# An S4D convolution beside a 16-head attention on one core: weights loaded by kind, one set of seeds kept on chip, step sizes multiplied in by diagonals

## The chip, the cores and the metric

The kernel runs on one core of one Trainium2 chip, in one launch. The metric is the device time in microseconds (us); where a kernel was run several times it is the median. The core's engines have short names throughout: PE (TensorE, the matrix unit, whose weight loads are listed apart as PEld), DVE (VectorE), ACT (ScalarE), POOL (GpSimd) and SP (SyncE, which issues most DMAs). [...]

## What is computed

Two independent results for a sequence of L = 2048 positions and D = 448 channels are put side by side.

```python
def _A_ref(u, log_A_real, A_imag, C_real, C_imag, log_dt, D_skip):     # N = 256 states per channel
    dt = jnp.exp(log_dt)
    A = -jnp.exp(log_A_real) + 1j * A_imag
    C = (C_real + 1j * C_imag) * dt[:, None]
    P = jnp.exp((A * dt[:, None])[:, :, None] * pos[None, None, :])
    K = 2.0 * jnp.einsum("dn,dnl->dl", C, P).real
    # y = causal convolution of u with K along L, by FFTs of 2 L
    return y + u * D_skip
def _B_ref(x, wqkv, wo):                                               # H = 16 heads of 28
    q, k, v = split(x @ wqkv)
    p = softmax(q k^T * 28 ** -0.5)
    return (p v) @ wo
out = concatenate([_A_ref(...), _B_ref(...)], axis=-1)
```

## The kernel before

All matmuls of the projections and scores run in fp32r on pairs of numbers, a rounded part ("hi") and its remainder ("lo"), so that three products (hi hi, hi lo, lo hi) come close to fp32. Every engine call goes through one helper (line 75), so the profile shows the same line for all instructions and is read by tiles. Up to the main loop a scheduler decides the order of the instructions; in the main loop they keep the order in which the program issues them (`KEPT`, lines 87, 93 and 903).

**Projections and seeds** (lines 226 to 575). The 448 columns of x are cut into four slices of 112 (`CK`, `NCK`). For each of four chunks of 512 rows, `transposes` turns x on PE (tile `pt`), ACT writes the rounded part `xh`, DVE the remainder `xl`. `qk_proj` makes eight products per chunk (four head groups, K and Q) and `v_proj` four, each of 4 slices x 3 matmuls into one PSUM tile `pm`; ACT and DVE then write hi and lo (`hl`, for Q of the last chunk into `xn`), which go to DRAM. The weights come in four DMAs, one per slice, with Q, K and V side by side (`tri`, lines 305 to 311); ACT and DVE split them into hi and lo, in the space that K of group 0 takes later (`w_g` in `k0_t`, tile `khat`).

Between the projections run the seeds of the convolution, `seeds(o)`, for eight sets of 56 channels. A set's four parameter blocks land in `nat` (56 x 4 x 256); ACT takes the exponential of the first and multiplies all four with the step sizes (`times_dt`, one instruction each); `turn` transposes them in eight pieces into one PSUM tile `pn`; phases, sizes and sines follow (tile `tri`), then powers of the states in `se` (stored from a buffer of tile `qhat`, 896 KB a set) and `sg` (1456 KB a set). `factors` ends with negated copies, three ACT instructions per call, two calls a set. `put_e` and `put_g` store a set to DRAM (`sd`). The stores of set 6 (`kept_e`, `kept_g`) are issued after the last projection, around the loads of v and of q.

**First maxima** (lines 576 to 589). The softmax needs a row maximum for each query. For the first unit of queries (head group 0, chunk 0) 16 groups of four matmuls are made here, into five PSUM tiles; ACT takes a relu of one per group, DVE the maxima. `max_end` turns the result (tile `mh`) and `max_put` writes it with two DMAs into two spare rows of `q_u[0]`, so that the score matmul subtracts the maximum by itself. These two DMAs are on ACT's queue.

**Hand-over** (lines 903 to 910). Three loads of `sdb` (one channel block of 336 KB each) are issued, one on ACT's queue, then the maxima of the first three groups of the next unit (`LEAD` = 3, twelve matmuls through three PSUM tiles), called the lead here, then the first seeds are copied (`k_seeds`).

**Main loop** (lines 1045 to 1102). 256 steps: 16 units of 512 queries by one head group, 16 blocks of 128 keys. `ORDER` (line 34) writes out what a step issues: four score matmuls `s` (tile `pss`, exponentials on ACT into `p`), four maxima matmuls `m` for the step 19 ahead, the product with v of the step before (`pv`, tile `po`), slots `f` for the convolution, and `v` and `k`, which build the convolution's kernel from the seeds (`e_power` on POOL, `g_powers` on DVE, block b from step 3.5 b on). K of the next head group is loaded in four pieces at steps 1, 5, 9 and 13 of a group's second unit (line 1066), into `k0_p` and `kq_p` by turns.

Of the kernel before, what the change touches and what calls it, by code (L numbers as in the profile page):

```python
# [17 lines left out]
L = 2048  # L18
D = 448
# [8 lines left out]
CK = 112  # L28
NCK = D // CK
# [12 lines left out]
SGB, XB, XL = 2, 5, 4  # L42
# [10 lines left out]
NO = 8  # L53
BO = NB // NO
# [36 lines left out]
def body(ctx, tc, a, out):  # L91
# [50 lines left out]

    kt_g, kd_g, q_u, m_u, mh_u, o_u, rl_u = {}, {}, {}, {}, {}, {}, {}
# [82 lines left out]
    with ExitStack() as st:  # L226
        sst, xst, wst = ExitStack(), ExitStack(), ExitStack()
        t_p = pool(sst, "t_p")
# [19 lines left out]
        def load_nat(o, queue=nc.sync):  # L248
            nats[o] = s_p.tile([PO, 4, 256], F32, name="nat", bufs=2)
# [4 lines left out]
        dt_all = s_p.tile([PO, 5, NO], F32, name="dt_all")  # L254
        small = s_p.tile([128, BO, SDF - F_G], F32, name="sg", bufs=SGB)
# [6 lines left out]
        load_nat(0, nc.scalar)  # L262
# [27 lines left out]
        def turn_dt():  # L290
            dt_ps = ps_t.tile([128, CQ], F32, name="pt")[:PO, :NO]
            nc.tensor.transpose(dt_ps, dt_o, ident[:NO, :NO])
            for i, f in enumerate((1.0, 0.15915494309189535, 2.0, -2.0, -1.0)):
                nc.vector.tensor_scalar(dt_all[:, i, :], dt_ps, f, None, op0=ALU.mult)

        load_x(0)
        w_g = k0_t[:CK].rearrange("p g (i s k h e) -> p i s k g h e", i=2, s=2, k=NCK, h=HG)
        vh = y_p.tile([CK, NCK, D], F32R, name="vh")
        vl = y_p.tile([CK, NCK, D], F32R, name="vl")
        nc.gpsimd.memset(k0_t[:CK].rearrange("p g (n e) -> p (g n) e", e=32)[:, :, DH:].bitcast(F32), 0.0)  # L300
# [5 lines left out]
        for i in range(2):  # L306
            wn = t_p.tile([128, 3, LV, BO * 16], F32, name="tri", bufs=2).rearrange("p t k h -> p (t k h)")
            wn = wn[:CK, :2 * 3 * D].rearrange("p (k s d) -> p k s d", k=2, s=3)
            wns += [wn[:, 0], wn[:, 1]]
        for k in range(NCK):  # L310
            nc.sync.dma_start(wns[k], wqkv[k * CK:(k + 1) * CK, :].rearrange("p (s d) -> p s d", s=3))
# [5 lines left out]
        for k in range(NCK):  # L317
            for s in (1, 0):
                src = wns[k][:, s, :].rearrange("p (g h e) -> p g h e", g=G, e=DH)
                hi, lo = (w_g[:, i, s, k, :, :, :DH] for i in range(2))  # L320
                nc.scalar.activation(hi, src, AF.Copy)
                nc.vector.tensor_tensor(lo, src, hi.bitcast(F32), ALU.subtract)
            nc.scalar.activation(vh[:, k, :], wns[k][:, 2, :], AF.Copy)
            nc.gpsimd.tensor_tensor(vl[:, k, :], wns[k][:, 2, :], vh[:, k, :].bitcast(F32), ALU.subtract)
# [6 lines left out]
        def seeds(o):  # L331
# [53 lines left out]
            def places():  # L385
                se = q_p.tile([128, HG, CQ], F32R, name="qhat", bufs=3).bitcast(F32).rearrange("p h q -> p (h q)")
                q["se"] = se = se[:, :BO * F_G].rearrange("p (b f) -> p b f", f=F_G)
                q["sg"] = sg = s_p.tile([128, BO, SDF - F_G], F32, name="sg", bufs=SGB)
                q["e8"] = se.rearrange("p b (c h e) -> p b c h e", c=2, e=8)
# [779 lines left out]
```

## Time and profile before

| | us |
|---|---|
| median of 3 runs (1276.06 to 1277.42) | 1276.75 |
| the profiled execution | 1278.37 |
| its span, first to last instruction | 1276.6 |
| PE busy in the span | 1223.9 |
| DVE, ACT, POOL busy | 923.0, 967.5, 846.2 |

The profile is of one execution. A row of a group gives engine, operation, output and input tiles with their shapes and the count, then busy time and mean duration in ns, then the engine's idle time before these instructions and who ended it. A row of the timeline gives start, duration, engine, operation and tiles, with an idle time before it in brackets. The granted clock is the share of full speed that PE's clock had. Matmuls overlap in the array, so that their pace is read from their starts and not from their durations.

### The profile page before, as it was taken

The numbers are of one execution on the slowest core, as the hardware profiler recorded it, in microseconds if no ns is written. First come the engines' busy times: TensorE is split into PE (matmuls) and PEld (weight loads), VectorE is DVE, ScalarE is ACT, GpSimd is POOL, SyncE is SP. The second block draws the span as 40 slices with busy tenths as digits, with TensorE's granted clock in tenths as the row PEclk, the third lists the DMA queues.
The fourth block names the chain that finished last, engine by engine and source line by source line (L and its number), as shares of the span: only waits on it lengthen the run. The fifth ranks groups of instructions, "written<-read, shape, count | busy, mean of one in ns | idle before, by whom it ended". The sixth has DMA issues, their size and how long they took to land.

```text
span 1276.6 us, 33328 instructions
## 1 busy us (share of the span) xinstructions
PE 1223.9 (96%) x12641; PEld 699.3 (55%) x12641; DVE 923.0 (72%) x2106; ACT 967.5 (76%) x2162; POOL 846.2 (66%) x728
## 2 busy tenths in 40 slices
PE   7789887999999999999999999999999999999997
PEld 5667664555555555555555555555555545544433
DVE  6788866877777877877788888888897645645111
ACT  6878765788888888888878888888887666656452
POOL 2666750897788888878599999989995222324321
PEclk9889999899999999999999999999999999999999
DMA  7768699446564645375633133422324533657666
GB/s 216 244 223 288 233 304 346 113 93 186 160 149 113 168 119 168 113 235 167 176 94 104 49 88 97 154 81 71 88 54 156 179 131 135 204 170 228 198 170 167
DMA packets 200089, 205.36 MB, mean 161 GB/s; under 512 B 95992, under 2 KB 158520, under 8 KB 197880
## 3 DMA queue, kind: packets, MB, share of 16 engines
q1 hardware_dynamic: 199400, 202.63, 52.6%
q8 instruction: 100, 1.64, 0.5%
q10 hardware_dynamic: 528, 0.59, 0.2%
q14 instruction: 61, 0.50, 0.1%
HBM read 120.73 MB, written 82.18 MB: 159 GB/s over the span
## 4 chain that ended last, share of the span: by engine, by line
PE 75%; DVE 8%; POOL 6%; ACT 4%; issue 3%; DMA 3%; SPq 0%; ACTq 0%; POOLq 0%; DVEq 0%
PE pm L75 43%; PE pss L75 16%; PE po L75 16%; POOL e L75 2%; DVE tri L75 1%; ACT rl L75 1%; POOL qhat L75 1%; DVE mx L75 1%; DVE sg L75 1%; POOL eu L75 1%; ACT tri L75 1%; DVE px L75 1%; DVE qhat L75 1%; DVE hl L75 1%; DMA sd<-qhat 1%
## 5 line engine op out<-in xcount | busy, mean ns | idle before, releaser
L75 ACT ACTIVATE p<-pss 128x512 f32<-128x512 f32 x1024 | 561.0, 610 | 112.5 <-PE pss L75 107.2
L75 PE MATMUL pss<-qhat,khat 128*128 128x512 f32 x1024 | 403.2, 400 | 1.5 <-ACT p L75 1.4
L75 DVE TENSOR_REDUCE mx<-pm 128x1 f32<-128x512 f32 x480 | 308.6, 684 | 109.1 <-PE pm L75 107.2
L75 PE MATMUL pm<-khat,qhat 128*128 128x512 f32 x749 | 325.9, 438 | 6.4 <-ACT rl L75 4.2
L75 POOL TENSOR_TENSOR e<-e,sdb 128x256 f32<-128x256 f32 x168 | 201.8, 1201 | 110.6 <-ACT e L75 101.2
L75 PE MATMUL po<-p,v 128*32 128x512 f32 x2048 | 269.1, 594 | 0.0
L75 POOL TENSOR_TENSOR e<-e,eu 128x256 f32<-128x256 f32 x168 | 248.2, 1477 | 13.2
L75 PEld LDWEIGHTS pm<-khat,qhat 128*128 128x128 f32 x749 | 141.0, 189 | 201.9 <-ACT p L75 47.8
L75 DVE CUSTOM_DVE_ANT_0 rl<-pm,rl 128x512 f32<-128x512 f32 x259 | 178.3, 689 | 72.1 <-ACT rl L75 69.1
L75 PEld LDWEIGHTS pss<-qhat,khat 128*128 128x128 f32 x1024 | 190.6, 189 | 46.7 <-issue 10.8
L75 POOL TENSOR_TENSOR eu<-e,sdb 128x256 f32<-128x256 f32 x168 | 201.9, 1202 | 0.0
L75 POOL TENSOR_TENSOR p<-pr,pr 64x448 f32<-64x448 f32 x64 | 73.2, 1144 | 158.2 <-PE pm L75 132.8
L75 ACT ACTIVATE rl<-pm 128x512 f32<-128x512 f32 x259 | 156.6, 606 | 14.0 <-PE pm L75 8.4
L75 DVE TENSOR_TENSOR g<-g,zg 128x128 f32<-128x128 f32 x392 | 162.2, 414 | 3.4
L75 PE MATMUL pm<-kdif,qhat 128*128 128x512 f32 x249 | 100.5, 403 | 4.3 <-DVE xn L75 2.4
L75 PE MATMUL pm<-xh,khat 112*128 112x512 f32 x256 | 87.3, 425 | 4.9 <-DVE hl L75 1.8
L75 DVE TENSOR_TENSOR zg<-g,zg 128x128 f32<-128x128 f32 x224 | 88.0, 393 | 5.1
L75 PEld LDWEIGHTS pm<-e,g 128*32 128x32 f32 x3584 | 57.2, 109 | 43.4 <-issue 17.1
L75 DVE TENSOR_TENSOR pr<-pm,ub 128x448 f32<-128x448 f32 x64 | 37.0, 620 | 56.4 <-PE pm L75 42.0
L75 PE MATMUL pm<-e,g 128*32 128x64 f32 x3584 | 73.0, 222 | 1.8 <-POOL e L75 1.8
L75 ACT ACTIVATE y<-pm 128x448 f32<-128x448 f32 x48 | 26.5, 553 | 58.2 <-PE pm L75 36.2
L75 ACT ACTIVATE ub<-pm 128x224 f32<-128x224 f32 (+1 forms) x96 | 38.8, 449 | 39.7 <-PE pm L75 37.3
(134 smaller groups left out, 1461.8 us busy)
## 6 DMA issues: line engine op xcount, KB each, us to landing
sdb<-sd SPq DMA_DIRECT2D x55, 336.0 KB
qhat<-q SPq DMA_DIRECT2D x64, 256.0 KB
khat<-k SPq DMA_DIRECT2D x64, 256.0 KB
sd<-sg SPq DMA_DIRECT2D x8, 1456.0 KB
k<-hl SPq DMA_DIRECT2D x16, 512.0 KB
mw<-in_mw SPq DMA_DIRECT2D x16, 512.0 KB
sd<-qhat SPq DMA_DIRECT2D x8, 896.0 KB
yu_d<-ub SPq DMA_DIRECT2D x64, 112.0 KB
```

The costliest lines, as they stand in the source:

```text
L75: i = f(*args, **kw)
```

## The change

- The slices become three of 128 columns and one of 64 (`CK`, `TL`). In the last slice the 64 columns stand twice: x and its weights are loaded into both halves, DVE turns the lower half of `xh` into remainders, and so `w_hi` and `w_lo` times that tile are two matmuls and no third.
- The weights are loaded by kind, K first, then Q, then V, five DMAs each, and split in that order ahead of the jobs of the first chunk, whose four K projections stand first.
- The seeds' sets run in the order 1 to 7, 0. Set 0 stays in SBUF, in a tile `k1_p` of K's size that is allocated from the start (it replaces the odd groups' place in `kq_p` and holds `nat`, `sg` and the diagonals meanwhile); its seven blocks are read from there, and neither stored nor loaded. The stores of set 7 and three loads of v stand behind the row of maxima, which is now on SP's queue. Loads of the next K come 8 steps later (`KL`).
- The lead's matmuls stand behind the row too, in twelve allocations over `pm`, `pt`, `pn` and `px`, and step 0 has an order of its own.
- `times_dt` keeps one ACT multiplication (the phases); DVE makes four diagonals `dg` of step sizes, and `turn` multiplies three blocks by them while turning: fp32 products in the place of six transposes.
- The three negated copies of `factors` are one instruction.

```diff
-CK = 112
-NCK = D // CK
+CK = 128
+NCK = 4
+TL = D - 3 * CK
+ORDER_0 = ('s0', 's1', 's2', 'k', 's3', 'm0', 'm1', 'v', 'f', 'f', 'v', 'm2', 'm3', 'v')
+KL = 8
-SGB, XB, XL = 2, 5, 4
+XB, XL = 5, 3
+SETS = (1, 2, 3, 4, 5, 6, 7, 0)
+ORDER_QK = tuple((g, s) for g in range(4) for s in (1, 0))
...
+        k1_f = k1_p.tile([128, HG * L], F32, name="khat")
+        n_g, n_n = BO * (SDF - F_G), 4 * 256
+        sg_at = (0, HG * L - n_g)
...
-                xns[c, h] = y_p.tile([128, 2, CQ], F32, name="xn", bufs=3)[:, :, :D]
-                nc.sync.dma_start(xns[c, h], xs[:, 2 * h:2 * h + 2, :])
+                xns[c, h] = y_p.tile([128, 2, CQ], F32, name="xn", bufs=3)
+                for d, n, at in ((0, D, 0), (D - TL, TL, D)):
+                    nc.sync.dma_start(xns[c, h][:, :, at:at + n], xs[:, 2 * h:2 * h + 2, d:d + n])
...
-        for k in range(NCK):
-            nc.sync.dma_start(wns[k], wqkv[k * CK:(k + 1) * CK, :].rearrange("p (s d) -> p s d", s=3))
+        for s in (1, 0, 2):
+            for k in range(NCK):
+                for p in range(1 if k < NCK - 1 else 2):
+                    n = CK if k < NCK - 1 else TL
+                    nc.sync.dma_start(wns[s][p * TL:p * TL + n, k], wqkv[k * CK:k * CK + n, s * D:(s + 1) * D])
...
-            def times_dt(i):
-                n, d = q["nat"][:, i, :], dt_all[:, i or 4, o:o + 1]
-                act.activation(n, n, AF.Copy, scale=d)
+            def times_dt():
+                n = q["nat"][:, 1, :]
+                act.activation(n, n, AF.Copy, scale=dt_all[:, 1, o:o + 1])
+                vec.tensor_tensor(dg, ident[:PO, None, :PO].to_broadcast([PO, 4, PO]),
+                                  dt_all[:, :, o][:, :, None].to_broadcast([PO, 4, PO]), ALU.mult)
...
-                        nc.tensor.transpose(ps[:, i, :, h, :], q["nat"][:, i, h * 128:(h + 1) * 128], ident[:PO, :PO])
+                        n = q["nat"][:, i, h * 128:(h + 1) * 128]
+                        if i == 1:
+                            nc.tensor.transpose(ps[:, i, :, h, :], n, ident[:PO, :PO])
+                        else:
+                            nc.tensor.matmul(ps[:, i, :, h, :], n, dg[:, i].rearrange("p (b e) -> p b e", e=8), start=True, stop=True)
...
-                for k in range(i, i + 3):
-                    act.activation(zz[:, k, :, n_, :], zz[:, k, :, p_, :], AF.Copy, scale=-1.0)
+                act.activation(zz[:, i:i + 3, :, n_, :], zz[:, i:i + 3, :, p_, :], AF.Copy, scale=-1.0)
...
-                xl[k] = x_p.tile([CK, CQ], F32R, name="xl", bufs=XL)
-                nc.vector.tensor_tensor(xl[k], pt, xh[k].bitcast(F32), ALU.subtract)
+                if k < NCK - 1:
+                    xl[k] = x_p.tile([CK, CQ], F32R, name="xl", bufs=XL)
+                    nc.vector.tensor_tensor(xl[k], pt, xh[k].bitcast(F32), ALU.subtract)
+                else:
+                    nc.vector.tensor_tensor(xh[k][TL:], pt[TL:], xh[k][TL:].bitcast(F32), ALU.subtract)
...
-                for i, x_ in ((0, xh), (1, xh), (0, xl)):
+                for i, x_ in ((0, xh), (1, xh), (0, xl))[:3 if k < NCK - 1 else 2]:
...
-                kept_e.pop()()
                 load_q(1)
-                for c in range(1, NQ):
-                    load_v(0, c)
-                kept_g.pop()()
...
-        max_put(0, nc.scalar)
+        max_put(0)
+        for c in range(1, NQ):
+            load_v(0, c)
+        for f, in kept:
+            f()
+        late_w = [w_tile] * 3 + [p_t, p_n, p_n, p_x, p_t, p_n, p_n, p_x, p_t]
+        for i in range(LEAD):
+            for kc in range(4):
+                max_mm(1, i, kc, late_w[4 * i + kc])
...
+    for b in range(BO):
+        sds[b] = se_view[:, b], sg_view(1)[:, b]
...
-    for b in range(3):
-        load_sd(b, nc.sync if b else nc.scalar)
-    for i in range(LEAD):
-        for kc in range(4):
-            max_mm(1, i, kc)
...
-        if kt % 4 == 1 and u % NQ == 1 and u // NQ + 1 < G:
-            load_k(u // NQ + 1, kt // 4, k_pools[(u // NQ + 1) % 2])
+        uk, kk = divmod(s - KL, NK)
+        if kk % 4 == 1 and uk >= 0 and uk % NQ == 1 and uk // NQ + 1 < G:
+            load_k(uk // NQ + 1, kk // 4, k_pools[(uk // NQ + 1) % 2])
...
-        for op in ORDER:
+        for op in ORDER if s else ORDER_0:
```

More of the change, by code (lines that the diff above doesn't have):

```diff
@@ L456, in load @@
                 q["nat"] = nats.pop(o)
-            dts = lambda *r: [lambda i=i: times_dt(i) for i in r]
             fa, fb = lambda: factors(0, 3, 2, 1), lambda: factors(3, 8, 1, 2)
-            return [[load], [exp_a] + dts(1, 2, 3), dts(0), [turn], [phases, sizes], [reduce], [sines], [g_base],
+            return [[load], [exp_a], [times_dt], [turn], [phases, sizes], [reduce], [sines], [g_base],
                     [places, fa, e_base], [e3, g_first], [fb, e5, g_copies], [put_g], [put_e]]
@@ L513, in v_proj @@
             for k in range(NCK):
-                for w_, x_ in ((vh, xh), (vl, xh), (vh, xl)):
-                    nc.tensor.matmul(pp[:, :D], x_[k][:, ts], w_[:, k, :], start=n == 0, stop=n == 3 * NCK - 1)
+                for w_, x_ in ((vh, xh), (vl, xh), (vh, xl))[:3 if k < NCK - 1 else 2]:
+                    nc.tensor.matmul(pp[:, :D], x_[k][:, ts], w_[:, k, :], start=n == 0, stop=n == 3 * NCK - 2)
                     n += 1
@@ L532, in body @@
             work += jobs
-        stages = [seeds(o) for o in range(NO)]
+        stages = [seeds(o) for o in SETS]
         n_stage = SP * (NO - 1) + len(stages[0]) - SH
         slots = [[] for _ in range(n_stage)]
-        kept_g, kept_e = (stages[NO - 2][i] for i in (-2, -1))
-        stages[NO - 2][-2:] = []
+        kept = stages[-2][-2:]
+        stages[-2][-2:] = stages[-1][-2:] = []
         for o in range(NO):
@@ L601, in body @@
     ps_w[0] = pool(ps_st, "ps_m", 1, PSUM)
-    k_pools = [k0_p, kq_p]
+    k_pools = [k0_p, k1_p]
     late = [False]
@@ L653, in body, with load_sd @@
     sds, egs = {}, {}
-    def load_sd(b, queue=nc.sync):
-        sds[b] = g_p.tile([128, SDF], F32, name="sdb", bufs=4)
-        queue.dma_start(sds[b], sd_d[b // BO][b % BO])
+    def load_sd(b):
+        if b >= BO:
+            t = g_p.tile([128, SDF], F32, name="sdb", bufs=4)
+            sds[b] = t[:, :F_G], t[:, F_G:]
+            nc.sync.dma_start(t, sd_d[b // BO][b % BO])
+    for b in range(BO):
+        sds[b] = se_view[:, b], sg_view(1)[:, b]
     def k_seeds(b):
```

76 lines of the change are left out of this document (47 added, 29 removed).

## The prediction

> **What bounds the kernel now.** First the page: the span, the busy rows and TensorE's forty slices.
>
> ```profile
> span 1276.6 us, 33328 instructions
> PE 1223.9 (96%) x12641; PEld 699.3 (55%) x12641; DVE 923.0 (72%) x2106; ACT 967.5 (76%) x2162; POOL 846.2 (66%) x728
> PE   7789887999999999999999999999999999999997
> ```
>
> TensorE (PE) is full everywhere but in the first seven slices, some 220 us, so I cut the span into stages: start (to 12.6 us), projections with seeds, first maxima, hand-over to the main loop, main loop, end. The columns of the view by stages: width, busy time of PE, weight loads, DVE, ACT, POOL, granted clock, DMA share, GB/s.
>
> ```profile
> 12.60:187.20 174.60, 156.16 (x690) 123.12 (x688) 139.73 (x264) 138.09 (x339) 105.71 (x133) 0.93 0.76 251
> 187.20:219.30 32.10, 24.93 (x82) 14.62 (x83) 22.94 (x68) 21.23 (x39) 1.45 (x2) 0.95 0.96 347
> 219.30:231.00 11.70, 8.90 (x21) 5.11 (x20) 7.13 (x17) 4.16 (x10) 3.27 (x5) 0.56 0.81 248
> 231.00:1220.00 989.00, 982.05 (x11336) 534.27 (x11334) 737.82 (x1712) 775.38 (x1724) 720.26 (x567) 1.00 0.47 136
> ```
>
> The main loop runs PE at 982 of 989 us: no edit takes work from PE there, so it can move but not shrink. What can shrink lies before 231 us. In the stage of the projections PE is busy 89%, DVE 80%, ACT 79%, and the clock is 0.93, that is 0.07 x 174.6 = 12 us lost. Whom PE waited for in that stage, and one wait of POOL (us, times, longest):
>
> ```profile
> PE pm L75 <- DVE hl L75: 6.8, 6, 2.6
> PE pt L75 <- DVE xl L75: 5.0, 4, 2.7
> PE pn L75 <- ACT nat L75: 3.0, 2, 2.8
> ...
> POOL qhat L75 <- DMA sd<-qhat: 6.2, 2, 4.2
> ```
>
> So PE sets the pace, and DVE is the next behind it.
>
> **The change, part by part.** Durations are of the profiled execution (1278.37 us with what lies around its span, 1.6 above the median of 1276.75); I work out a difference and take it from the median.
>
> 1. *Slices of 128 instead of 112.* Each projection has 11 matmuls instead of 12, as the last slice carries 64 columns of x and, below them, their remainders. 32 projections of 512 columns and 16 of 448 lose one each. Their pace, from starts in the timeline:
>
> ```profile
> 28.02 0.40 PE L75 MATMUL pm<-xl,khat 112*128 112x512 f32 x1
> 28.26 0.62 PE L75 MATMUL pm<-xh,khat 112*128 112x512 f32 x2
> 28.72 0.40 PE L75 MATMUL pm<-xl,khat 112*128 112x512 f32 x1
> ...
> 100.84 0.37 PE L75 MATMUL pm<-vh,xh 112*128 112x448 f32 x1
> 101.05 0.37 PE L75 MATMUL pm<-vl,xh 112*128 112x448 f32 x1
> ```
>
> Three take 28.72 - 28.02 = 0.70, so 0.233 each, and one of 448 columns 0.21: 32 x 0.233 + 16 x 0.21 = **10.8 us** off PE. 128 rows for 112 cost nothing: the main loop's 128-row matmuls of 512 columns start 0.23 apart too (237.39 and 237.62, quoted in part 5). DVE keeps its four remainders per chunk; the fourth has half the partitions and the same 512 columns. The small second load of x per half is eight more issues on SP, which has gaps there: 0.
>
> 2. *Step sizes by diagonals.* Of the four scalings per set ACT keeps one; DVE builds one 56x224 product; six of the eight transposes become fp32 products.
>
> ```profile
> L75 ACT ACTIVATE nat<-nat,dt_all 56x256 f32<-56x256 f32 x32 | 14.8, 505 | 0.0
> L75 ACT ACTIVATE sg<-sg 128x112 f32<-128x112 f32 x48 | 10.8, 294 | 0.0
> L75 ACT ACTIVATE e<-sdb 128x256 f32<-128x256 f32 x56 | 24.5, 438 | 0.0
> L75 DVE TENSOR_TENSOR px<-pn,gz 128x224 f32<-128x224 f32 x16 | 6.2, 390 | 0.1
> L75 PE MATMUL po<-p,v 128*32 128x512 f32 x2048 | 269.1, 594 | 0.0
> ...
> 21.78 0.70 PE L75 MATMUL pn<-ident,nat 56*128 56x56 f32 x8
> ```
>
> ACT: 24 x 14.8/32 = 11.1 us less. DVE: 8 x 0.39 = 3.1 more. PE: eight transposes take 0.70, 0.0875 each. The kernel issues 1024 products into po and the trace has 2048 matmuls, so an fp32 product runs as two. At the transposes' pace a product is 0.175: 48 x 0.0875 = **4.2 us** more on PE. From below the extra is 0 (the second pass hidden whole), from above two passes with nothing overlapped, each 0.138 for the weights and 0.223 for the matmul:
>
> ```profile
> L75 PEld LDWEIGHTS pn<-ident,nat x64: 134/138/142, 21.8 to 155.4; 56*128 56x128 f32 x64
> L75 PE MATMUL pn<-ident,nat x64: 221/223/267, 21.8 to 155.4; 56*128 56x56 f32 x64
> ```
>
> That is 0.72, or 48 x (0.72 - 0.0875) = 30 us. I take 4.2, as weights and matmuls do overlap in the row of eight.
>
> [...]
>
> 3. *Negated copies joined.* 48 copies at 10.8/48 = 0.225 become 16 of 336 elements, a little over the 256-element row's 24.5/56 = 0.44: I take 0.48, and 10.8 - 7.7 = 3.1 us leave ACT. With part 2 ACT has 14 us less of 138. ACT is not the bound; what this buys is PE's waits for nat (3.0) and an earlier hl, kb and tri for DVE. Next late is DVE (hl, xl), which has 3 us more to do. I count **1.5 us** of the 3.0, with bounds of +1 (DVE gives it all back) and -9 (half of PE's 18.4 idle us go).
>
> 4. *Weights by kind.* PE begins after the K weights, a third of the bytes. But from 12.6 us on PE lacks little today, as three accumulations run slice by slice while weights arrive:
>
> ```profile
> 12.60:30.00 17.40, 17.02 (x75) 12.87 (x74) 11.82 (x24) 12.92 (x36) 5.46 (x6) 1.00 0.72 203
> ```
>
> I count **0**, bounds -2 (earlier start) and +1 (fifteen issues instead of four on SP, and ACT's four copies of V now stand ahead of the first hl).
>
> 5. *Hand-over.* The row of maxima leaves by ACT's queue, and ACT is then busy issuing:
>
> ```profile
> 219.34 0.28 DVE L75 SCALAR_TENSOR_TENSOR mh<-pt,mh 16x128 fp32r<-16x128 f32 x1
> 222.70 0.69 DVE L75 CUSTOM_DVE_ANT_0 rl<-pm,rl 128x512 f32<-128x512 f32 x1 [3.09 <-ACT rl L75]
> ...
> 219.38 2.01 ACTq L75 DMA_DIRECT2D qhat<-mh  x2
> 221.43 0.60 ACTq L75 DMA_DIRECT2D sdb<-sd  x1
> 222.07 0.60 ACT L75 ACTIVATE rl<-pm 128x512 f32<-128x512 f32 x1 [4.46 <-issue]
> ...
> 222.72 0.79 PE L75 MATMUL pm<-khat,qhat 128*128 128x512 f32 x1 [2.80 <-ACT rl L75]
> ...
> 228.65 0.63 PE L75 MATMUL pss<-qhat,khat 128*128 128x512 f32 x1
> ...
> 237.39 0.40 PE L75 MATMUL pm<-kdif,qhat 128*128 128x512 f32 x1
> 237.62 0.39 PE L75 MATMUL pss<-qhat,khat 128*128 128x512 f32 x1
> ...
> 238.54 0.96 PE L75 MATMUL pm<-ua,w 128*32 128x448 f32 x8
> ...
> 0.74 1.79 DMA ident<-in_ident
> ```
>
> With the row on SP's queue ACT can take the lead's first relu when PE has made it, at about 219.4, and the lead's twelve matmuls no longer share three PSUM tiles. DVE's first maximum of the lead then starts at 219.4 + 0.6 + 0.1 = 220.1 instead of 222.7, 2.6 us earlier. The row lands near 223 (219.6, then two issues in up to the 2.0 that ACT took, and 1.8 from issue to landing, the first load's time in the chain). Scores 0 to 3 follow, where today the first stands at 228.65 behind the lead. Step 1 of the main loop (231.0 today) comes **3.5 us** earlier: DVE's 2.6, and 0.9 of the time that this stage loses at clock 0.56 (0.44 x 11.7 = 5.1). Bounds: -7.7 (2.6 and all of the 5.1) and -1.5 (the row lands 2 us later, since scores now wait for it with nothing ahead). Queued behind that wait on SP: three loads of v, the two kept stores, u's loads; v's next block is wanted only at step 4.
>
> 6. *Set 0 kept: its two stores and seven loads gone.* The one wait on such a store is POOL's (6.2 us, above), and POOL is busy 106 of 175 us there: 0, as PE covers it. The later load of the next K (by 8 steps) has 20 steps until its first use: 0. Main loop 0, bounds of 2 either way.
>
> **Sum:** -10.8 + 4.2 - 1.5 + 0 - 3.5 = **-11.6 us**; 1276.75 - 11.6 = 1265.2.
>
> **Rivals.** (1) *DVE paces the projections.* For it: PE's longest waits are for DVE's hl and xl, and DVE gains 3 us. Against it: PE is 89% busy, DVE 80%, and DVE itself waits for ACT, which is relieved. Then parts 1 to 3 bring only about 1 us and the hand-over 3.5: -4.5, **1272**.
>
> (2) *A product costs four transposes, not two.* The chain of work shows the array's side:
>
> ```profile
> 243.00 0.86 PE po L75 x8
> ```
>
> Four fp32 products stand side by side there, in two passes of 512 columns: 0.86 against 0.233, 3.7 times. If that applies to the whole 0.0875, each product is 0.35, 12.6 us in all instead of 4.2: -3.2, **1273.5**. Against it: at 56 columns the array needs 56/512 x 0.86 = 0.09, and a transpose at 0.0875 is three times what its 56 columns take (56/512 x 0.233 = 0.025), so something other than the array bounds it. [...]
>
> (3) *u's loads come late behind the stores.* On SP's queue three loads of v and the two kept stores stand ahead of them:
>
> ```profile
> sd<-sg SPq DMA_DIRECT2D x8, 1456.0 KB
> sd<-qhat SPq DMA_DIRECT2D x8, 896.0 KB
> v<-v SPq DMA_DIRECT2D x16, 256.0 KB
> ```
>
> That is 3120 KB, 3.2 MB; at the maxima's 347 GB/s it takes 9.2 us from 221 on, until 230, and u's first matmul comes near 235 (238.54 less 3.5). Below 230 GB/s PE stands: some 3 us, **1268**.
>
> (4) *Slower: the products run unoverlapped.* In place of the 4.2 PE gets 30: +14, **1291**. It decides from 0.41 us per product on (10.8 + 1.5 + 3.5 = 15.8 us over 48, on top of 0.0875). Against it: the row of eight transposes at 0.70.
>
> That the change does nothing is out: matmuls leave the program.
>
> **Chances.** Forecast 0.58; (1) 0.18; (2) 0.12; (3) 0.05; (4) 0.07. A measurement of this kernel tells about 0.2%, 2.6 us, from no change, so faster means below 1274.2. (1) and (3) lie there, (2) half: 0.87 faster, 0.06 the same, 0.07 slower. The range takes in (1) to (3) and the bounds: at the low end -9 for the waits in place of -1.5 gives 1257.7, and more of the hand-over's clock would add to it; at the high end rival (2) is 1273.5. I give 1256 to 1274.
>
> **What would show it.** Projections of 11 matmuls at 0.23; eight pn instructions giving 14, in about 1.2 us (2.5 would be rival 2, 4.5 rival 4); projections ending near 179 instead of 187.2, with PE's wait for nat gone; if PE's waits for hl and xl grow instead, rival 1. In the hand-over: DVE without the 3.09 gap, the first scores near 215 (223 less 8). The main loop from its step 1 to the end as long as today, 1045 us; if it differs by over 2 us, my reading that nothing there moves is wrong.

## The result, and the profile after

The change makes the kernel slightly slower: 1281.0 us (median of 20 runs, 1277.2 to 1289.4) against 1278.2 (20 runs, 1276.1 to 1280.9) on the same chip. The ratio is 1.0026 with an interval of 1.0017 to 1.0036, so +3.3 us (2.2 to 4.6). Forecast were -11.6. The profiled execution took 1282.58 us. Its page has these rows, to be read beside those of before:

```profile
span 1280.8 us, 33305 instructions
PE 1222.2 (95%) x12641; PEld 699.6 (55%) x12641; DVE 924.9 (72%) x2113; ACT 955.6 (75%) x2106; POOL 844.9 (66%) x728
PE   6898888899999999999999999999999999999997
```

The span is 4.2 us longer. ACT lost 12 us of work and DVE gained 2, near the 14 and 3 forecast; PE lost 1.7 where 6.6 were forecast. The next view cuts the span into stages: projections; first maxima; hand-over up to step 1 of the main loop; from there to the first matmul on u, the convolution's input; main loop. Its columns are those of the prediction.

```profile
12.60:191.95 179.35, 154.35 (x688) 124.11 (x686) 141.70 (x270) 125.65 (x285) 106.74 (x134) 0.92 0.73 244
191.95:222.09 30.14, 24.12 (x81) 13.23 (x80) 22.22 (x66) 21.05 (x37) 0.00 (x0) 1.00 0.68 250
222.09:230.94 8.85, 6.71 (x22) 3.58 (x22) 6.83 (x17) 5.05 (x11) 4.78 (x6) 1.00 0.59 205
230.94:242.49 11.55, 10.39 (x36) 5.06 (x36) 9.19 (x21) 5.71 (x12) 8.62 (x7) 0.70 0.79 254
242.49:1220.00 977.51, 969.98 (x11248) 529.04 (x11251) 726.27 (x1686) 766.50 (x1706) 709.14 (x558) 1.00 0.46 135
```

The projections end at 191.95, where before the first maxima begin at 186.77: 5.2 us later, not 8 earlier. The first maxima then take 30.14 us instead of 31.95 (186.77 to 218.72). Hand-over and the first main-loop steps together take 20.40 us; before they took 19.82:

```profile
218.72:231.00 12.28, 9.48 (x22) 5.47 (x23) 7.41 (x17) 4.16 (x10) 3.27 (x5) 0.58 0.82 255
231.00:238.54 7.54, 7.54 (x38) 3.61 (x36) 7.40 (x19) 6.69 (x15) 7.30 (x5) 1.00 0.53 181
```

From u's first matmul to the end it is 1280.8 - 242.49 = 1038.3 us against 1276.6 - 238.54 = 1038.1. So all of the loss lies ahead of u's first matmul: the projections lose 5.2 us, the first maxima give 1.8 back, and the hand-over loses 0.6. The next rows say whom PE waited for in the projections of the kernel after, with one wait of DVE; the last row is that wait of DVE in the kernel before.

```profile
PE pm L80 <- DVE hl L80: 8.5, 6, 3.0
DVE tri L80 <- PE pn L80: 6.4, 5, 2.2
PE pm L80 <- ACT vst L80: 4.3, 2, 3.1
PE pm L80 <- DVE kb L80: 3.7, 1, 3.7
```

```profile
DVE tri L75 <- PE pn L75: 2.7, 1, 2.7
```

PE has less to do per projection and waits more for its PSUM tiles, those that its matmuls write, to be read (by the instructions that write hl, vst and kb): 8.5, 4.3 and 3.7 us, where before it was 6.8, 1.1 and 1.4. DVE now waits 6.4 us for PE's turn of the seeds instead of 2.7.

### The profile page after: what moved, and what is told of

It is laid out like the page before. It is cut to its first block, busy times and chain, and to the rows that moved or that the text cites. A ratio compares the mean times of both kernels' runs of the same rounds, so it can differ in the third digit from the quotient of the medians.

```text
span 1280.8 us, 33305 instructions
## 1 busy us (share of the span) xinstructions
PE 1222.2 (95%) x12641; PEld 699.6 (55%) x12641; DVE 924.9 (72%) x2113; ACT 955.6 (75%) x2106; POOL 844.9 (66%) x728
## 4 chain that ended last, share of the span: by engine, by line
PE 77%; DVE 9%; POOL 4%; ACT 4%; issue 3%; DMA 2%; SPq 0%; ACTq 0%; POOLq 0%; DVEq 0%
PE pm L80 44%; PE pss L80 16%; PE po L80 16%; POOL e L80 1%; DVE khat L80 1%; DVE tri L80 1%; DVE mx L80 1%; ACT rl L80 1%; DVE px L80 1%; PE pt L80 1%; ACT p L80 1%; ACT tri L80 1%; POOL p L80 1%; POOL qhat L80 1%; DVE rl L80 1%
## 5 line engine op out<-in xcount | busy, mean ns | idle before, releaser
L80 DVE TENSOR_REDUCE mx<-pm 128x1 f32<-128x512 f32 x475 | 305.3, 683 | 111.6 <-PE pm L80 109.4
L80 PE MATMUL pm<-khat,qhat 128*128 128x512 f32 x742 | 321.5, 435 | 5.6 <-DVE mx L80 3.1
L80 POOL TENSOR_TENSOR e<-e,sdb 128x256 f32<-128x256 f32 x147 | 176.7, 1202 | 64.1 <-ACT e L80 56.0
L80 POOL TENSOR_TENSOR eu<-e,sdb 128x256 f32<-128x256 f32 x147 | 176.8, 1203 | 0.0
L80 PE MATMUL pm<-xh,khat 128*128 128x512 f32 x256 | 87.1, 432 | 12.0 <-DVE hl L80 5.2
```

The lines of the kernel that those rows point to most:

```text
L80: i = f(*args, **kw)
```

## The experiments

Each kernel was timed in five rounds beside the kernel before on the same chip. A difference to before is (ratio - 1) x 1278.2 us; a ratio is good to about 0.0011, so a single difference to about 1.4 us and one between two such differences to about 2.

### One part undone at a time (e1 to e3), slices alone (e4)

There were four theories at this point. A: the order of the first chunk (K first, V's weights ahead of the evacuations, that is, of the copies of finished PSUM tiles) starves PE. B: PE does not pace the projections, so matmuls that go become idle time. C: the diagonals, with their longer turn, cost the time. D: what the hand-over gains is given back a few steps later.

e1 has the weights loaded and split slice by slice again, and K and Q by turns in the first chunk.

```diff
-        for s in (1, 0, 2):
-            for k in range(NCK):
-                for p in range(1 if k < NCK - 1 else 2):
+        for k in range(NCK):
+            for p in range(1 if k < NCK - 1 else 2):
...
-            jobs = [lambda c=c, s=s, g=g: qk_proj(c, s, g) for g, s in (ORDER_QK if c else sorted(ORDER_QK, key=lambda o: -o[1]))]
+            jobs = [lambda c=c, s=s, g=g: qk_proj(c, s, g) for g, s in ORDER_QK]
```

> The changed kernel with the weights loaded and split slice by slice again, and K and Q alternating in the first chunk as in the others; slices of 128, diagonals, hand-over as changed. Theory A (the order of the first chunk costs: PE's wait of 3.75 us at 22.8 to 26.5 and half pace behind it, c0 5.8 us longer than before): the first chunk's last V matmul ends near 50 instead of 55.9 and the kernel takes about 5 us less than the changed one, 1276. Theory B (PE is paced by ACT and DVE through the whole stage, so a gain in one chunk is lost in the next): the first chunk is faster but the projections still end near 191, total 1280 to 1281. Theory C (the diagonals' products and their waits cost the time): 1281, within 1.

Measured 1283.3, ratio 1.0033 (1.0021 to 1.0044): 0.9 us slower than the change, inside the uncertainty. **A falls**: the 5 us that it expected from the old order are not there.

e2 has four ACT scalings and eight transposes per set again.

```diff
-            def times_dt():
+            def times_dt(i):
...
-                            nc.tensor.matmul(ps[:, i, :, h, :], n, dg[:, i].rearrange("p (b e) -> p b e", e=8), start=True, stop=True)
+                        nc.tensor.transpose(ps[:, i, :, h, :], q["nat"][:, i, h * 128:(h + 1) * 128], ident[:PO, :PO])
```

> The changed kernel with the step sizes multiplied in by four ACT scalings per set and eight transposes again; all else as changed. Theory C (each set's turn takes 1.6 us instead of 0.70 on PE, eight sets, and PE's turn waits for DVE's diagonals): 7 us less, 1274. Theory B (ACT paces; the scalings are 11 us of ACT work more): same or up to 3 us more, 1281 to 1284. Theory A: same within 1, and the first chunk as long as in the changed kernel (last V matmul near 56).

Measured 1276.1, ratio 0.9983 (0.9974 to 0.9991): 5.5 us less than the change, and a little faster than before. C holds in sign; its size comes below.

e3 has the row on ACT's queue, and the lead, the kept stores and the loads of v at their old places.

```diff
-        max_put(0)
+        max_put(0, nc.scalar)
...
-        for op in ORDER if s else ORDER_0:
+        for op in ORDER:
```

> The changed kernel with the row of maxima on ACT's queue, the lead's matmuls behind it through three PSUM tiles, the kept stores and loads of v ahead of the first maxima, and the old order of step 0; set 0 is still kept on chip. If the changed hand-over gained 3.5 us, as forecast, this takes 3.5 more: 1284.5. Theory D (the hand-over gained nothing, since the clock's drop only moved to 233 to 239): within 1 of the changed kernel, with the time from the last maxima's transpose to u's first matmul at 19.8 against 20.4.

Measured 1280.3, ratio 1.0018 (1.0007 to 1.0028): 1.0 us less than the change, not more. The new hand-over brings nothing, as D has it, though the last transpose stands 17.9 us ahead of u's first matmul here, not the 19.8 expected.

e4 is the kernel before with slices of 128 and nothing else.

```diff
-CK = 112
-NCK = D // CK
+CK = 128
+NCK = 4
+TL = D - 3 * CK
```

> The kernel before with slices of 128 and nothing else of the change (PE loses 48 matmuls, 10.8 us of its pace; weights by slice, old turn, old hand-over). The forecast's first term: 10.8 us less than before, 1267. Theory B (PE is not what paces the projections: fewer matmuls become idle time, and the clock falls after longer idle time): within 2 of before, 1276 to 1280, with PE busy less and its idle time more by about 10 in the projections. Theories A and C say nothing against 1267.

Measured 1282.7, ratio 1.0033 (1.0021 to 1.0045). The part that should bring 10.8 us costs 4.2 by itself, more than B allowed. On B's clause about the clock: in e4's profile it is 0.50 from 59 to 62 us, after 2.80 us without a matmul (until 58.16), but 1.00 after 2.88 us (until 128.55).

### The same order of instructions (e5 to e8)

Between before and e4 the scheduler had changed the order on every engine: in e4, for example, six of ACT's eleven exponentials of the first set of seeds (tri) stand ahead of its first evacuation (hl), where before all eleven stand behind the first three. So in the next runs the order is held, by an edge from each instruction to its predecessor on its engine, in the order wanted, up to the main loop:

```diff
+        for e, o in order.items():
+            of = [i for i in traced if str(i.engine).endswith(e) and type(i).__name__ != "BassTilePoolBoundary"]
+            for p, n in zip(o, o[1:]):
+                tc.add_manual_dep(of[n], of[p].name, mybir.DependencyInfo(
+                    mybir.DependencyClass.NoSync, mybir.DependencyReason.DATA), reason="hold")
```

e5 is e4 in the order of before (theory S: the order costs; B as above).

> The kernel of e4 (before, with slices of 128 and nothing else), but every engine's instructions up to the main loop held in exactly the order that they have in the kernel before (each instruction queued behind the one that stood before it there; the 48 missing matmuls left out, the nine more loads right behind their partners). Theory S (the scheduler, given other matmul counts, puts the seeds' work of ACT and DVE ahead of the evacuations, and this order is what costs): the forecast's first term comes back, 1267 to 1271. Theory B (ACT and DVE pace the stage whatever the order; fewer matmuls only become idle time): 1276 to 1283.

e6 is the reverse, before in the order of e4.

> The reverse: the kernel before, unchanged, with its 12 matmuls per projection, but held in the order that e4 has on every engine (the twelfth matmul right behind the eleventh). Theory S: the order costs by itself, so this is at least as slow as e4, 1283 to 1293 (e4's 1282.7 plus up to the 10.8 of the 48 matmuls). Theory B (the matmuls fall into idle time, nothing hangs on the order): 1277 to 1280, as before.

e5: 1280.6, ratio 1.0021 (1.0011 to 1.0030), +2.7 us. e6: 1284.9, ratio 1.0055 (1.0042 to 1.0068), +7.0. Both theories hold in part. S: unchanged work in another order costs 7 us. B: in the order of before, the slices bring nothing. In e5's profile the time without a busy PE between 12 and 245 us is 40.8 us instead of 28.4, 12.4 more: what was taken from PE became waiting. Why e5 is even slower is the question of e14. In e4's order the slices do bring something: e4 is 2.8 us below e6 (4.2 and 7.0). So what they are worth hangs on the order too, and in neither order is it 10.8.

What the holding itself costs was not measured, as no run holds the kernel before without another edit. Comparisons of two held kernels (e5, e7, e8, e10, e11, e14 among each other) do not need it; those of a held kernel with before (e5, e6, e9, e13, e14) contain it.

e7 adds the diagonals to e5, e8 the joined copies, both in the same order.

```diff
+        dg = s_p.tile([PO, 4, PO], F32, name="dg")
...
-            return [[load], [exp_a] + dts(1, 2, 3), dts(0), [turn], [phases, sizes], [reduce], [sines], [g_base],
+            return [[load], [exp_a, times_dt], [], [turn], [phases, sizes], [reduce], [sines], [g_base],
```

> The kernel of e5 with the diagonals added (one ACT scaling per set for four, 48 fp32 products for transposes), held in the same order; each set's diagonals stand on DVE right behind the phases of the set before. Against e5: theory C (a turn takes 1.6 us instead of 0.70 on PE, all of it on the path) 7 us slower; the forecast's terms (4.2 for the products, -1.5 for ACT's relief) 2.7 slower; if PE has idle time enough and ACT is what paces, the same or up to 5 faster.

> The kernel of e5 with the three negated copies of a set's factors joined into one instruction (32 ACT instructions fewer, 3.1 us of ACT by the forecast), held in the same order. Against e5: 0 to 1 us faster if ACT is not on the path, as the forecast has it; 3 faster if ACT paces the stage (theory B).

e7: 1285.6, ratio 1.0058 (1.0045 to 1.0070), 4.7 us above e5, between the 2.7 of the forecast's terms and the 7 of theory C. e8: 1279.1, ratio 1.0010 (1.0001 to 1.0019), 1.4 below e5, between the two expectations and within the uncertainty of either. The view of tile pn, e5 and then e7:

```profile
L76 PE MATMUL pn<-ident,nat x64: 221/223/352, 22.1 to 158.0; 56*128 56x56 f32 x64
...
  ACT nat L76: 3.0, 2
...
  DVE tri L76: 2.6, 2
```

```profile
L76 PE MATMUL pn<-dg,nat x96: 272/272/459, 22.2 to 163.6; 56*128 56x56 f32 x96
L76 PE MATMUL pn<-ident,nat x16: 221/222/227, 22.7 to 162.8; 56*128 56x56 f32 x16
...
  DVE tri L76: 7.0, 4
```

PE's wait for nat is gone, as forecast, but DVE waits longer for the turn. One of e7's turns, from 141.95 to the next projection at 143.55, is 1.6 us where eight transposes take 0.70 (the 48 products show as 96 matmuls, two each, as the prediction read from po):

```profile
141.95 0.65 PE L76 MATMUL pn<-dg,nat 56*128 56x56 f32 x4
142.44 0.28 PE L76 MATMUL pn<-ident,nat 56*128 56x56 f32 x2
142.57 1.05 PE L76 MATMUL pn<-dg,nat 56*128 56x56 f32 x8
143.55 0.48 PE L76 MATMUL pm<-vh,xl 128*128 128x448 f32 x1
```

Six products take 1.67 (to the end of the last) - 2 x 0.0875, so 0.25 each. With the order equal, DVE's instructions can be laid beside each other: up to the fifth turn e7 is 1.6 us behind e5, through waits elsewhere; then it falls back in steps at DVE's first reading of pn, by 0.9, 1.5 and 1.2 us for the fifth, seventh and eighth set, and by 1.0 to 1.3 where DVE waits for the projections behind the sixth turn; some of it is caught up between. So the lengthened turn (by 0.97 us) counts nearly in full in the second half of the sets.

### What paces the projections (e9 to e11, e13)

The chain of waits follows the work that ended last back in time, from each instruction to what released it. Cut to the projections of the kernel before, it has these pieces, among others, in order of time (start, us, what):

```profile
25.66 1.45 DVE tri L75
27.14 1.58 ACT tri L75 x10
28.76 0.51 ACT dhl L75
29.34 0.88 POOL dhl L75
30.21 3.82 issue
34.06 1.00 POOL gz L75
35.06 1.16 POOL qhat L75 x3
36.23 1.28 POOL dhl L75
37.53 2.17 DMA kd<-dhl
39.70 0.66 DVE hl L75
```

For 14 us the chain runs through DVE, ACT, POOL and a store, and PE is not in it, though PE is busy for 13.82 us of that time. Added up by engine, the 195 longest pieces of the stage make 171.0 us: DVE 62.9, PE 28.2, POOL 27.0, ACT 19.5, DMA 16.7, issue 12.9, SP's queue 3.8. The new theory B: a chain from set to set of the seeds, and from evacuation to evacuation, paces the stage.

e9 takes 43 us from PE, estimated from the paces that the prediction read (128 x 0.233 + 64 x 0.21), and from nobody else.

```diff
-                for i, x_ in ((0, xh), (1, xh), (0, xl)):
+                for i, x_ in ((0, xh), (0, xl)):
```

> The kernel before, slices of 112, held in its own order, but without the product of the remainders of the weights with the rounded x: 8 of 12 matmuls per projection, so 192 matmuls less, some 43 us off PE (128 x 0.233 + 64 x 0.21). Left out: that product; the results are less exact. Nobody's waits change but those for PE. If PE paces the projections, as the forecast had it, the time falls by about 30 us, to 1248 (until DVE, busy 140 of 175 us, is full). Theory B in its new form (a chain through the seeds on DVE, POOL and ACT paces the stage; of the chain of waits in this stage PE holds 28 of 171 us): 0 to 10 us less, 1268 to 1278.

Measured 1274.1, ratio 0.9969 (0.9958 to 0.9979): -4.0 us for 192 matmuls. Its projections, and whom PE waits for in them:

```profile
12.60:180.65 168.05, 131.04 (x496) 98.38 (x496) 139.40 (x264) 136.81 (x339) 105.56 (x133) 0.81 0.76 252
```

```profile
PE pm L75 <- DVE hl L75: 15.7, 10, 3.0
```

The stage is 6.1 us shorter, not 30. PE is still busy for 131 us: at a granted clock of 0.81 instead of 0.93 a matmul takes 0.26 us of busy time on average (131.04 / 496) where before it took 0.23 (155.76 / 690). It waits for hl 15.7 us instead of 6.8. The lower clock is a rival here: by an estimate from the two clocks it loses 0.19 x 168 = 32 us where before lost 12, and may have eaten a part of the gain. e5 beside e14 (below) is free of this: the clock in 12.6 to 180 us is 0.94 and 0.92, and 10.8 us less on PE still bring only 0.2.

e13 takes 51 us from POOL, which is busy only 60% there.

```diff
-            e5 = lambda: cmul(pol, e8(5, 8), e8(1, 4), 3, q["e8"][:, :, 0, :, 4], q["e8"][:, :, 1, :, 4], False)
+            e5 = lambda: [pol.memset(t, 0.0) for t in e8(5, 8)]
```

> The kernel before, held in its own order, with POOL's last products of each set's seeds (six TENSOR_TENSORs of 336 elements, some 7 us a set) replaced by two memsets to zero. Left out: the powers 5 to 7 of the states, so the convolution's result is wrong. POOL has some 50 us less to do in a stage where it is busy 106 of 175 us, PE, DVE and ACT have the same. If a chain through the seeds paces the stage (POOL holds 27 of the 171 us of the chain of waits): 5 to 20 us less, 1258 to 1273, more than the 192 matmuls of e9 brought (4.1). If only the busiest engines count (PE, DVE, ACT, all above 79%): 0 to 2 less.

Measured 1272.5, ratio 0.9953 (0.9941 to 0.9966): -6.0 us, at the small end of what the chain allowed and out of reach of "only the busiest engines count":

```profile
12.60:179.36 166.76, 152.65 (x692) 121.43 (x690) 133.01 (x263) 137.15 (x340) 54.88 (x102) 0.96 0.77 257
```

So neither PE nor POOL paces the stage. 43 us off the busiest engine bring 4.0, 51 us off the least busy one 6.0 (the two differ by no more than the uncertainty); each holds only its part of the chain. DVE holds the largest part, 62.9 of 171.0 us, and no run took work off DVE.

e10 and e11 take the 4.7 us of the diagonals apart: DVE's work for them without their use, and a longer turn without them.

```diff
-            return [[load], [exp_a] + dts(1, 2, 3), dts(0), [turn], [phases, sizes], [reduce], [sines], [g_base],
+            return [[load], [exp_a] + dts(1, 2, 3) + [spare], dts(0), [turn], [phases, sizes], [reduce], [sines], [g_base],
...
-                for i in range(4):
+                for i in [*range(4)] * 2:
```

> The kernel of e5 (1280.6) with the eight products that build the diagonals on DVE, at the place that they have in e7, but nobody uses them: the turn is the old one. DVE 3.1 us more, PE and ACT as in e5. If DVE's time is on the path one for one: +3, 1283.7; if the 5.0 us of the diagonals (e7 against e5) come from the products on PE: 0 to +1.

> The kernel of e5 with the eight transposes of each set's turn made twice, the second time over the first: about 0.70 us more per set on PE, 5.6 in all, no fp32 product, no diagonal. If the turn stands in the chain of the seeds, whatever it consists of: +4 to +6, 1285 to 1287. If PE has idle time to take it (as it took the 10.8 us of the slices): 0 to +1.

e10: 1281.4, ratio 1.0022 (1.0012 to 1.0032), 0.1 us above e5: the eight instructions on DVE cost nothing clear of noise at their place. (This does not say that DVE is off the path elsewhere.) e11: 1280.2, ratio 1.0026 (1.0013 to 1.0039), 0.6 above e5. Its turns grew by 0.50 (1.20 for 0.70), not by 0.70; four of them in the chain would be 2.0, all eight 4.0. The uncertainty of 2 us does not tell 0.6 from 2.0, so e11 does not settle how many turns count; it speaks against all eight.

### Why the slices cost, and a faster version (e12, e14 to e18)

e14 is before, held, with nothing but the small second loads of x.

```diff
+                for d, n, at in ((0, D, 0), (D - 64, 64, D)):
+                    nc.sync.dma_start(xns[c, h][:, :, at:at + n], xs[:, 2 * h:2 * h + 2, d:d + n])
```

> The kernel before, held in its own order, with the extra loads of x that the slices of 128 need (64 columns per half chunk, eight small DMAs on SP's queue), into columns that nobody reads. If these loads make e5 2.5 us slower than before: +2 to +3, 1280.5. If the fourth remainder, which DVE now writes into the tile that the matmuls of the last slice read, or the missing matmuls do it: 0 to +0.5.

Measured 1280.9, ratio 1.0023 (1.0014 to 1.0032): +2.9 us, all of e5's loss and more. The start of the timeline, before and then e14:

```profile
1.20 0.98 SPq L75 DMA_DIRECT2D xn<-in_B_x  x2
...
2.54 5.36 SPq L75 DMA_DIRECT2D tri<-in_B_wqkv  x4
...
10.27 1.04 ACT L75 ACTIVATE khat<-tri 112x448 fp32r<-112x448 f32 x2 [1.30 <-DMA tri<-in_B_wqkv]
```

```profile
1.20 2.27 SPq L75 DMA_DIRECT2D xn<-in_B_x  x4
...
5.17 2.62 SPq L75 DMA_DIRECT2D tri<-in_B_wqkv  x4
...
7.77 0.69 PEld L75 LDWEIGHTS pt<-ident,xn 128*112 128x112 f32 x4 [1.82 <-DMA xn<-in_B_x]
...
11.74 1.04 ACT L75 ACTIVATE khat<-tri 112x448 fp32r<-112x448 f32 x2 [2.17 <-DMA tri<-in_B_wqkv]
```

Two small DMAs stand ahead of the weights: the weights are issued 2.6 us later, ACT gets them 1.5 later, x's second half is turned from 7.77 (weight loads; before from 5.81), and the evacuations stay 1.3 to 1.5 us late from the first (23.37 for 21.90) to the last of DVE's (186.32 for 185.03). So the trace follows 1.3 us to the end of the projections. The two profiled executions differ by 1.75 us (1280.12 and 1278.37), so the 2.9 of the medians is not seen whole in a trace. The start also scatters from execution to execution: the first projection starts at 10.94 to 11.45 us in the three kernels with this order and no small loads (before, e9, e13) and at 11.34 to 12.46 in the six with them (e5, e7, e8, e10, e11, e14).

e5 less e14 leaves -0.2 us for the 48 matmuls and the remainder written in place. No run parts these two. The remainder in place brings a wait that before does not have, 5.2 us in three pieces of PE for DVE's part of xh; by e9's rate (4.0 for 43) 10.8 us off PE would be worth 1.0.

e12 joins e2 and e3. e15 takes e2 with the old lead, row and step 0, but leaves loads of v and stores behind the row. e16 is e2 with the sets started closer together in the program, and the early loads of the first maxima moved with them.

```diff
-SP, SH, PW, E3 = 4, 3, 37, 8
+SP, SH, PW, E3 = 3, 3, 30, 8
...
-A0, A1 = 26, 31
+A0, A1 = 21, 25
```

> The changed kernel with both the old turn (e2) and the old hand-over (e3). If the parts add up: 1276.1 - 0.7 = 1275.4, faster than before by 0.2%. If the order that the scheduler makes of it decides more than the parts do, it lies anywhere in 1273 to 1282.

> The changed kernel with the old turn (e2, 1276.1) and, of the old hand-over, the row on ACT's queue, the lead through three PSUM tiles behind it and the old order of step 0; the loads of v and the kept stores stay behind the row, set 0 stays on chip. If set 0 kept is what helps (no loads of seeds on ACT's queue ahead of the lead) and the new order of the lead gives it back: about 18 us instead of 19.1 from the last transpose to u's first matmul, 1275. If the lead's new order gains: 1277 to 1279.

> e2 (the changed kernel with the old turn) with a new set of seeds every three slots instead of four, the projections spread over 30 slots instead of 37, the early loads of the first maxima moved in proportion (slots 21 and 25 for 26 and 31). If the seeds' chain paces the stage and PE has time to spare, starting the sets earlier shortens it: 2 to 8 us less than e2, 1268 to 1274. If buffers or ACT and DVE's sum of work are the limit: 1275 to 1282.

e12: 1277.1, ratio 0.9990 (0.9981 to 0.9998). The parts do not add up; its first maxima start 1.7 us later than e2's (188.3 for 186.6). e16: 1276.6, ratio 0.9986 (0.9977 to 0.9995), as e2. The edit did not bring the sets forward: DVE first reads the last set's pn at 154.4 us, in e2 at 152.6. So whether an earlier start would help stays open. e15: 1274.6, ratio 0.9975 (0.9965 to 0.9984). Its hand-over, the last transpose, the first maxima of step 1, and u's first matmul:

```profile
216.84 0.27 PE L80 MATMUL pt<-ident,m 128*16 128x128 f32 x1 [1.73 <-DVE m L80]
...
227.03 0.39 PE L80 MATMUL pm<-kdif,qhat 128*128 128x512 f32 x1
...
234.71 0.96 PE L80 MATMUL pm<-ua,w 128*32 128x448 f32 x8
```

10.2 us to step 1 and 7.7 from there to u, 17.9 in all; before 12.3 and 7.5, in the change 8.9 and 11.6. With set 0 on chip ACT has no load of seeds to issue between the row and the lead's first relu (221.43 before). So with the old lead set 0 kept is worth some 1.9 us here (17.9, 18.2 and 17.9 in e3, e12 and e15 against 19.8; e17 and e18 below, with the same lead, have 17.9 and 19.5). With the new order of the lead it is 20.4 in the change and 19.1 to 19.3 in e1, e2 and e16, so most or all of it is taken back. This is read from spans of single executions; no run undoes set 0 alone.

e17 is e15 with the first chunk's small loads replaced by a copy on POOL, e18 has the copy in all chunks.

```diff
+                    if at and c == 0:
+                        nc.gpsimd.tensor_copy(xns[c, h][:, :, D:], xns[c, h][:, :, D - TL:D])
```

> The kernel of e15 (1274.6: as changed, with the old turn and the old lead), but in the first chunk of x POOL copies the last 64 columns on chip, where two small loads brought them. If the delay at the start is what the small loads cost: the second half of x is turned 1.5 to 2 us earlier, and the kernel takes 1.5 to 2.7 less than e15, 1272 to 1273. If the weights set the start (K's weights alone come first here): 0 to 0.5 less.

> e17 with POOL's copies in all four chunks, so no small loads of x at all. If only the start counts: as e17, within 1. If the later small loads delay SP's queue or the arrival of x too: 1 to 2 less than e17. If POOL, in the chain of the seeds, pays for the copies: 1 to 3 more than e17.

e17: **1272.7**, ratio 0.9953 (0.9940 to 0.9967): 6.0 us faster than before, 2.8 faster than e15. PE's first projection matmul starts at 9.29 (10.80 in e15, 10.99 before, 10.38 in the change). With e14 (2.9) this is the second run that puts the small loads at the start near 3 us, here without held order. e18: 1276.7, ratio 0.9988 (0.9979 to 0.9997), slower than e17 although it starts at 9.07. Its first maxima come 2.2 us later than e17's (185.27 for 183.05), and the hand-over takes 19.5 instead of 17.9. The copies stand on POOL, and the order is another one; which of the two it is stays open.

## Why the prediction was wrong

- **The step that failed is the first: "So PE sets the pace, and DVE is the next behind it".** It was read from busy shares (89, 80, 79%). The chain of waits in the same stage gives PE 28 of 171 us, and e9 shows what a microsecond of PE is worth there: 4.0 of 43. In place of PE's pace the runs show a chain through the seeds on DVE, POOL, ACT and the stores, in which PE holds a sixth. Of the -10.8 us there came -0.2 in the order of before (e5 less e14). PE's busy share of 89% did not tell what its work was worth, and the ranking by busy shares did not help either: POOL, the least busy (60%), gave no less in e13 (6.0 us) than PE in e9 (4.0).
- **"eight more issues on SP, which has gaps there: 0"** was the second fault: +2.9 us (e14) and 2.8 (e17 less e15). The gaps are there later; at the start the weights stand behind the small loads, and ACT waits for them (2.17 us in e14, 1.30 before).
- **The products.** Forecast 0.175 each, measured 0.25, 2.8 times a transpose at 0.0875, between the forecast and rival 2 (0.35). No run shows rival 2's factor of four: the po row gives 3.7 (0.86 against 0.233), the products of 56 columns 2.8. On PE that is 8 x 0.97 = 7.8 us more, in time 4.7 (e7) to 5.5 (e2). Not because PE paces: DVE waits for the turn in the later sets (7.0 us in e7, 2.6 in e5). (The turn of 2.5 us that the prediction gives for rival 2 should read 2.3: 6 x 0.35 + 2 x 0.0875.)
- **ACT's relief, -1.5.** The wait for nat went in e7, as said, and gave nothing there. In the change itself it stayed: PE waits 3.2 us ahead of the turns for ACT's work on `khat`, which is the tile that holds nat there. The joined copies brought 1.4 (e8), with an uncertainty of 2.
- **Weights by kind, 0.** Right within its bounds: undone it costs 0.9 (e1), with an uncertainty of 2, and the first projection starts at 10.38 instead of e1's 12.39.
- **The hand-over, -3.5.** Right up to step 1, which stands 8.85 us behind the last transpose instead of 12.28, so 3.4 earlier. Then it was given back: the prediction stopped at step 1 and did not ask who is late next. PE's rows and then DVE's, in the kernel after:

```profile
230.94 0.51 PE L80 MATMUL pm<-kdif,qhat 128*128 128x512 f32 x1 [0.23 <-DVE mx L80]
...
232.84 0.80 PE L80 MATMUL pm<-khat,qhat 128*128 128x512 f32 x1 [1.16 <-DVE mx L80]
...
234.00 1.94 PE L80 MATMUL po<-p,v 128*32 128x512 f32 x8
...
237.74 0.63 PE L80 MATMUL pm<-kdif,qhat 128*128 128x512 f32 x1
```

```profile
231.45 0.74 DVE L80 TENSOR_TENSOR g<-g,zg 128x128 f32<-128x128 f32 x2
232.10 1.28 DVE L80 TENSOR_REDUCE mx<-pm 128x1 f32<-128x512 f32 x2
```

  DVE takes step 0's maxima only behind its products for the convolution's kernel (`g`), PE waits for its tiles until 232.84, and from there to 239.0 its granted clock is 0.50; step 1 takes 6.8 us (230.94 to 237.74), before 3.1 (231.00 to 234.07). At half clock some 3.1 of these 6.2 us are lost, by an estimate: the low clock that the prediction wanted to save in the hand-over (0.56 before, 1.00 after) came back behind it.
- **Set 0 kept, 0**: undersized by some 1.9 us, if the spans of e3, e12 and e15 are read so; most of it was lost again to the lead's new order.
- **Main loop 0**: right from u's first matmul on (1038.1 and 1038.3). The prediction's own sign, from step 1 on within 2 us of before, fails with 1049.9 for 1045.6; 4.0 of these 4.3 us lie between step 1 and u's first matmul, as told above.
- **The rivals.** (1), that PE does not pace, was nearest in mechanism, but it named DVE alone. PE's wait for hl grew, its wait for xl fell from 5.0 to 1.8, and 3.1 us more on DVE cost 0.1 at their place (e10); whether less on DVE would help was not tried. (3) did not happen: u's first matmul waits for nothing. (4), the only one that led to slower, was far off at 0.25 per product: its 0.07 came true in sign and by another cause. The others left the kernel faster: (1) by keeping the hand-over's 3.5 us, (2) and (3) by keeping the 10.8 too.
- **Missing altogether: the order.** Up to the main loop a scheduler orders the instructions, and each edit made a new order; e6 shows one worth 7.0 us with no work changed. Summed up: +2.7 for the slices, +4.7 to 5.5 for the diagonals, -1.4 for the copies make 6.0 to 6.8; the measured 3.3 leave some -3 for the weights by kind, set 0 and the order together, which the runs do not part further. Such a sum is a rough one, as e12 shows that the parts do not simply add up.

## What to carry to other kernels

Read the chain of waits of the very stage that an edit touches before counting its instructions: a microsecond saved on an engine was worth somewhat less than that engine's share of the chain, 0.09 for a share of 0.16 on PE (e9) and 0.12 for 0.16 on POOL (e13), and the busy shares of 89% and 60% did not tell this. Where a scheduler orders the work, compare two kernels in the same order, or the order's own effect (up to 7 us here) passes for the edit's. At the start, and in a serial turn between engines, small things can count nearly in full: a longer turn did in the second half of the sets (e7), and two small loads ahead of the weights cost more (2.9 us, e14) than 48 matmuls brought (0.2, e5 less e14). And where an edit makes one stage earlier, ask which engine is late in the next.

## What the runs showed of the hardware

In these stretches of the kernel before, PE's granted clock fell to half after short idle times and stayed there for some microseconds. They lie around the longest gap of its projections (2.76 us, 52.0 to 54.8) and around 76 to 80 us:

```profile
50.00:52.00 2.00, 1.61 (x9) 0.87 (x7) 1.97 (x5) 2.00 (x4) 1.84 (x3) 1.00 0.00 0
52.00:54.00 2.00, 0.01 (x1) 0.00 (x0) 1.97 (x4) 1.89 (x4) 2.00 (x3) 1.00 0.12 40
...
56.00:60.00 4.00, 2.18 (x6) 1.16 (x4) 1.65 (x5) 1.89 (x6) 2.19 (x6) 0.52 1.02 348
60.00:66.00 6.00, 5.17 (x14) 4.21 (x15) 6.00 (x13) 4.01 (x13) 4.58 (x5) 0.50 0.90 278
...
76.00:80.00 4.00, 2.88 (x18) 1.76 (x16) 1.36 (x4) 3.06 (x7) 2.35 (x5) 1.00 0.55 192
80.00:83.00 3.00, 3.00 (x7) 2.35 (x8) 2.80 (x6) 2.32 (x8) 2.36 (x5) 0.50 1.03 371
```

After 2.8 us without work (and again 2.7 at 58.2) the clock is 0.5 for 10 us, from 56 on; after only 1.1 idle of 4 us it is 0.5 for 3. Idle time alone does not decide it: in the kernel after, 3.01 us without a matmul (until 148.47) leave it at 1.00, and in the first maxima there PE is idle for 6 of 30 us at a clock of 1.00. The change's runs also spread more than those of before, and with the clock: of its 20 runs the fastest (1277.2 us) had a mean granted clock of 0.991, the slowest (1289.35) 0.979. Which of the two brings the other is not shown.
